# A spectral mixing layer and two gated MLPs in one kernel: the bias added on VectorE, token chunks cut across both batches, waits moved

## The chip, the cores and the metric

One Trainium2 chip; the kernel runs on one core. The metric is the device time of one launch in microseconds (us), the median of the runs shown. Lower is better.

## What is computed

```python
B, N, D, FF = 2, 3008, 256, 1536
X  = np.fft.rfft(x, axis=1)                      # x: (2, 3008, 256)
Yr = X.real @ w_r - X.imag @ w_i + b_r
Yi = X.real @ w_i + X.imag @ w_r + b_i
Yr, Yi = (np.sign(v) * np.maximum(np.abs(v) - 0.01, 0.0) for v in (Yr, Yi))
y  = np.fft.irfft(Yr + 1j * Yi, n=3008, axis=1)  # then 6016 tokens of 256
h  = (sigmoid(y @ w_gate) * (y @ w_val)) @ w_out         # weights in float64
g  = h @ w2_gate
out = (g * sigmoid(g) * (h @ w2_val)) @ w2_out
```

## The kernel before, in words

The transform over 3008 = 47 x 64 positions is done with matmuls in three stages: a 47-point stage, a 64-point stage with the mixing matrices and the shrinkage, and the way back. Nearly every product is done with values split into a high and a low part (three matmuls: high by high, low by high, high by low), with one weight load per matmul.

**First batch** (`spectral_first`, to about 98 us). The 47-point stage ends in `zt`. Then twelve steps run in a software pipeline; step i issues, in this order on TensorE: four transposes of step i+1 (`turn`), the 64-point transform of step i (`forward`), half of the mixing of step i-1 (`mix`), the inverse transform of step i-2 (`inverse`), the other half of `mix`. One half of `mix_of` is 13 matmuls of 256 columns: twelve for the products, and before them one that multiplies a matrix of ones and zeros (`ones`) by a table holding the bias (`bmov`, L239), so that the bias stands in PSUM. `spectrum_parts` splits the spectrum (ScalarE makes the high part, VectorE the low part) and appends the negated first half to each; `shrink_of` then does the shrinkage from PSUM:

```python
nc.scalar.activation(y, pm, AF.Relu, bias=lam)
nc.vector.scalar_tensor_tensor(out=y, in0=pm, scalar=LAM, in1=y, op0=ALU.add, op1=ALU.min)
```

**Weights.** Each of the 12 hidden blocks of a gated MLP arrives as float64 bits (`raw`, three DMAs, two buffers) and is turned into float32 high and low parts by `from_float64`: two ScalarE and seven VectorE operations in five steps (L74 and L75; L77; L80 to L82; L85; L87). `advance(dec)` issues one step. The load of block f+2 is issued after the third step of block f.

**Gated MLPs.** The tokens are cut into chunks: per batch five of 512 and one of 448 columns, 12 in all. A unit is one chunk by one hidden block: `hidden` (12 matmuls into `pg`, then ScalarE `sg`, VectorE `h`, ScalarE `hh`, VectorE `hl`; in the second MLP one more VectorE operation on `sg`) and, two units later, `project` (6 matmuls into `po`). Chunks 0 and 1 of the first MLP go through their blocks in three runs (`TURNS`), while blocks are still being decoded and the rest of the first batch's way back and then the second batch's whole transform (`spectral_second`, one step per unit) run between the units. In the second batch the mixing uses the same `mix_of` and `shrink_of`.

**Order.** Up to the end of the first batch's way back the instructions of each engine stand in program order. From `open_order` on only SP, the queue of nearly all DMAs, keeps program order; the other engines are put in order by the framework's scheduler. Each engine executes its own list strictly in order. At the end, `turn_out` transposes each output chunk and stores it by rows; the last chunk is handled in two pieces, and three of its eight stores are issued by GpSimd (POOL).

Of the kernel before, what the change touches and what calls it, by code (L numbers as in the profile page):

```python
# [37 lines left out]
def tile_kernel(ctx, tc, x, w_r, w_i, b_r, b_i, wts, f1, f2, s2, i1, i1f, eye, one, out):  # L38
# [9 lines left out]
    x2T = [dram.tile([P, 2, N], F32, name=f"x2T{b}") for b in range(B)]  # L48
# [92 lines left out]
    ones = cp.tile([P, P], F32R, name="ones")  # L141
    bmov = cp.tile([P, 256], F32R, name="bmov")
# [3 lines left out]
    def load_tables(fp):  # L146
        wraw = fp.tile([P, 2, 2, 256], F32, tag="wraw", bufs=1, name="wraw")
        braw = fp.tile([P, 256], F32, tag="braw", bufs=1, name="braw")
        nc.gpsimd.memset(braw, 0.0)
        yield  # L150
        nc.sync.dma_start(wraw[:, 0], w_r.rearrange("(k p) e -> p k e", p=P))
        nc.sync.dma_start(wraw[:, 1], w_i.rearrange("(k p) e -> p k e", p=P))
        nc.sync.dma_start(braw[0:33:32, :], b_r.partition_broadcast(2))
        nc.sync.dma_start(braw[1:34:32, :], b_i.partition_broadcast(2))
        nc.sync.dma_start(f2s, f2)
        nc.gpsimd.dma_start(ones, one)
# [8 lines left out]
        nc.vector.tensor_copy(bmov, braw)  # L165
        nc.vector.tensor_tensor(bmov[32:34], braw[32:34], bmov[32:34], op=ALU.subtract)
# [5 lines left out]
    def warm(n):  # L172
        pw = ps_b.tile([P, 512], F32, tag="f", name=f"warm{n}")
        for i in range(n):
            nc.tensor.matmul(pw, idle[:, 0:P], idle, start=True, stop=True)


    def stage1(b, ps, fp, c0=0):
# [4 lines left out]
        def load(c):  # L183
            xr[c] = fp.tile([NJ, 2, 256], F32, tag="xr", bufs=3, name=f"xr{b}_{c}")
            nc.sync.dma_start(xr[c][0:80], xb[0:80, 2 * c:2 * c + 2, :])
            nc.sync.dma_start(xr[c][80:94], xb[80:94, 2 * c:2 * c + 2, :])
# [17 lines left out]
        yield True  # L204
# [16 lines left out]
    def spectrum_parts(b, i, xs, fp, bufs):  # L221
# [6 lines left out]
        nc.vector.tensor_scalar_mul(Xl[:, :, :, 128:192], Xl[:, :, :, 0:64], -1.0)  # L228
# [8 lines left out]
    def mix_of(pm, Xh, Xl, ks):  # L237
        for k in ks:
            ops = [(ones, bmov)]  # L239
# [15 lines left out]
    def spectral_first(zz, ps):  # L255
# [6 lines left out]
        with tc.tile_pool(name="z0", bufs=1, reuse_waits="tile") as z0:  # L262
# [8 lines left out]
            with tc.tile_pool(name="p1", bufs=1, reuse_waits="tile") as fp:  # L271
# [18 lines left out]
                warm(9)  # L290
                next(tables)
                for t, (p0, n) in enumerate(tasks):
# [18 lines left out]
                    if t == 3:  # L311
                        nc.sync.dma_start(eyes, eye)
                        load_table2(0, "s2c", s2, s2c, 2)
                        next(tables)
                        load_table2(0, "i1c", i1f, i1c, 3)
                        next(dec)
                next(tables)
            with tc.tile_pool(name="p2", bufs=1, reuse_waits="tile") as fp:
# [37 lines left out]
                def shrink(i, ks):  # L356
                    shrink_of(Y[i][:, ks], M[i][:, ks])
# [3 lines left out]
                load_table2(1, "s2c", s2, s2c, 2)  # L361
                load_table2(1, "i1c", i1f, i1c, 3)
                for i in range(NS + 1):
# [6 lines left out]
                    if 0 < i < last:  # L370
                        advance(dec, 1 + i % 2)
# [19 lines left out]
    def stage2(b, ps, fz):  # L391
# [20 lines left out]
        def parts(i):  # L412
            X[i] = spectrum_parts(b, i, X[i], fp, 2)
# [5 lines left out]
        def shrink(i):  # L419
            Y[i] = fp.tile([P, KP, 256], F32, tag="y", bufs=1, name=f"y{b}_{i}")  # L420
            shrink_of(Y[i], M.pop(i))
# [125 lines left out]

    pzs = ctx.enter_context(ExitStack())
# [7 lines left out]
    def load_fill(c):  # L556
        xb = x[1].rearrange("(j p) c -> j p c", p=PP)
        x1[c] = pz.tile([NJ, 2, 256], F32, tag="x1", bufs=E1, name=f"x1_{c}")
# [7 lines left out]
    def filled(c, copy):  # L566
        z1 = pz.tile([96, 2, 256], F32, tag="z1e", bufs=2, name=f"z1e_{c}")
# [28 lines left out]
    chunks = []  # L596
    for b in range(B):
        t = 0
        while t < N:
            chunks.append((b, t, min(TC, N - t)))  # L600
            t += TC
    po, turned = {}, []

    def load_x(m, ci):
        b, t0, tn = chunks[ci]
        xin = mp.tile([P, 2, TC], F32, tag="xin", bufs=1, name=f"xin{m}_{ci}")
        nc.sync.dma_start(xin[:, :, :tn], (xT, x2T)[m][b][:, :, t0:t0 + tn])
# [6 lines left out]
    def hidden(m, ci, f):  # L614
        b, t0, tn = chunks[ci]
# [22 lines left out]
    def project(m, ci, f, hh, hl):  # L638
        b, t0, tn = chunks[ci]
# [5 lines left out]
        nt = (tn + 127) // 128  # L645
        for d in range(2):
            for i, (w, v) in enumerate(((wh, hh), (wh, hl), (wl, hh))):
                nc.tensor.matmul(o[d][:, :tn], w[:, 4 + d, :], v[:, :tn],  # L648
                                 start=(first and i == 0), stop=(last and i == 2))
# [6 lines left out]
    def drain(m, ci, f, o):  # L656
        b, t0, tn = chunks[ci]
        nt = (tn + 127) // 128
# [7 lines left out]
        elif ci in part and m == 0:  # L666
# [3 lines left out]
            nc.sync.dma_start(x2T[b][:, :, t0:t0 + tn], xo[:, :, :tn])  # L670
        elif m == 0:
# [3 lines left out]
            nc.sync.dma_start(x2T[b][:, :, t0:t0 + tn], xo[:, :, :tn])  # L675


    def turn_out(ci, o):
        b, t0, tn = chunks[ci]
        end = ci == len(chunks) - 1  # L680
        ot = mp.tile([P, 2, TC], F32, tag="ot", bufs=1, name=f"ot{ci}")
        cut = 256 if end else tn
# [5 lines left out]
        dst = out[b * N:(b + 1) * N, :].rearrange("(j p) c -> p j c", p=PP)  # L688
        ob = mp.tile([P, 4, 256], F32, tag="ob", bufs=RC, name=f"ob{ci}")
        for j in range(0, tn, 256):  # L690
# [6 lines left out]
            for a, k in enumerate(js):  # L697
# [153 lines left out]
```

## Time and profile before

| what | value |
|---|---|
| runs | 1372.14, 1375.63, 1374.31 us; median 1374.31 us |
| profiled execution | 1373.79 us, span in the trace 1372.0 us |
| granted TensorE clock | 0.999 of full speed |
| TensorE (PE) busy | 1358.1 us, 99% of the span, 6814 matmuls |
| VectorE (DVE) busy | 722.1 us, 53% |
| ScalarE (ACT) busy | 536.3 us, 39% |
| GpSimd (POOL) busy | 10.7 us, 1% |
| DMA | 76.09 MB, mean 55 GB/s |

A matmul's recorded duration contains the latency of the array, and successive matmuls overlap; what one of them costs the engine is the distance from its start to the start of the next. A TensorE that is busy 99% can therefore still wait a little between two starts, and only the longer of these waits show as idle time. Each row of a group gives the instructions' busy time, their mean duration in ns, and the idle time of the engine ahead of them with what ended it.

### The profile page before, as it was taken

To read this page: it belongs to the slowest core of one execution; us is meant where nothing else is said; L and a number is where in the kernel's file an instruction comes from. 1 tells how busy PE (TensorE), PEld (TensorE's weight loads), DVE (VectorE), ACT (ScalarE), POOL (GpSimd) and SP (SyncE) were. 2 spreads that over 40 slices of the span, in tenths; PEclk is the share of its full clock that TensorE was granted. 3 is DMA by queue.
4 is the path that set the end of the run, shared out by engine and by line. 5 is a ranking of instruction groups with operands and counts; after the bars stand their busy time and mean duration, and the time that the engine had idled before them with its cause. 6 is when DMAs were issued, how large, how long until landed. Compare 5 with 4: busy or idle time off the path is not lost.

```text
span 1372.0 us, 16931 instructions
## 1 busy us (share of the span) xinstructions
PE 1358.1 (99%) x6814; PEld 1159.4 (85%) x6814; DVE 722.1 (53%) x1099; ACT 536.3 (39%) x941; POOL 10.7 (1%) x25
## 2 busy tenths in 40 slices
PE   9999999999999999999999999999999999999998
PEld 8988878998888888888888888888889888888887
DVE  3648884444334864633335755455555555555554
ACT  4655554444333443433233433333333333333332
POOL 0000000000000000000000000000000000000000
PEclk9999999999999999999999999999999999999999
DMA  7313333333232321000003001001101100100100
GB/s 206 99 56 109 119 111 112 94 108 112 88 109 81 100 75 53 25 31 31 0 29 100 29 1 31 20 13 31 29 0 32 29 4 27 31 11 21 29 15 15
DMA packets 59519, 76.09 MB, mean 55 GB/s; under 512 B 5769, under 2 KB 40632, under 8 KB 59441
## 3 DMA queue, kind: packets, MB, share of 16 engines
q1 hardware_dynamic: 57313, 71.51, 17.2%
q0 software_dynamic: 2128, 3.51, 1.2%
q8 instruction: 53, 0.87, 0.3%
q14 instruction: 25, 0.20, 0.0%
HBM read 51.27 MB, written 23.72 MB: 55 GB/s over the span
## 4 chain that ended last, share of the span: by engine, by line
PE 91%; DMA 3%; DVE 3%; ACT 1%; SPq 1%; issue 1%; POOL 0%; DVEq 0%; POOLq 0%; ACTq 0%
PE pg L623 52%; PE po L648 25%; PE pm L246 5%; PE p L489 2%; PE p L234 2%; PE p L297 1%; DMA raw<-in_moe_w_out_dram 1%; PE pt L696 1%; PE pi L343 1%; DMA xr<-in_x_dram 1%; PE pi L436 1%; PE p L478 1%; DMA xin<-x2T 1%; DMA xin<-xT 0%; PE p L211 0%
## 5 line engine op out<-in xcount | busy, mean ns | idle before, releaser
L623 PE MATMUL pg<-fxh,wh 128*128 128x512 f32 (+1 forms) x1152 | 447.0, 388 | 2.0 <-DVE h L631 1.0
L623 PE MATMUL pg<-fxh,wl 128*128 128x512 f32 (+1 forms) x1152 | 444.1, 386 | 2.1 <-DVE wl L87 2.1
L623 PE MATMUL pg<-fxl,wh 128*128 128x512 f32 (+1 forms) x1152 | 444.2, 386 | 0.0
L627 ACT ACTIVATE sg<-pg 128x512 f32<-128x512 f32 (+1 forms) x288 | 169.0, 587 | 358.0 <-PE pg L623 357.8
L634 ACT CAST hh<-h 128x512 fp32r<-128x512 f32 (+1 forms) x288 | 175.9, 611 | 309.4 <-DVE h L631 308.7
L631 DVE TENSOR_TENSOR h<-sg,pg 128x512 f32<-128x512 f32 (+1 forms) x288 | 194.3, 675 | 188.8 <-ACT sg L627 183.9
L636 DVE TENSOR_TENSOR hl<-h,hh 128x512 fp32r<-128x512 f32 (+1 forms) x288 | 195.6, 680 | 156.1 <-ACT hh L634 154.7
L623 PEld LDWEIGHTS pg<-fxh,wh 128*128 128x128 f32 x1152 | 216.4, 188 | 44.0 <-DVE h L631 2.5
L623 PEld LDWEIGHTS pg<-fxh,wl 128*128 128x128 f32 x1152 | 216.3, 188 | 43.1 <-DVE wl L87 2.5
L623 PEld LDWEIGHTS pg<-fxl,wh 128*128 128x128 f32 x1152 | 216.4, 188 | 38.7
L648 PE MATMUL po<-hh,wh 128*128 128x512 f32 (+1 forms) x576 | 223.9, 389 | 1.0 <-DVE part L661 0.9
L648 PE MATMUL po<-hl,wh 128*128 128x512 f32 (+1 forms) x576 | 222.1, 386 | 0.0
L648 PE MATMUL po<-hh,wl 128*128 128x512 f32 (+1 forms) x576 | 222.1, 386 | 0.0
L629 DVE TENSOR_TENSOR sg<-sg,pg 128x512 f32<-128x512 f32 (+1 forms) x144 | 97.3, 676 | 160.3 <-ACT sg L627 159.9
L648 PEld LDWEIGHTS po<-hh,wh 128*128 128x128 f32 x576 | 108.1, 188 | 21.3 <-DVE part L661 1.3
L648 PEld LDWEIGHTS po<-hh,wl 128*128 128x128 f32 x576 | 108.1, 188 | 20.4
L648 PEld LDWEIGHTS po<-hl,wh 128*128 128x128 f32 x576 | 108.2, 188 | 19.8 <-DVE hl L636 0.4
L246 PE MATMUL pm<-wmh,Xl 128*128 128x256 f32 x192 | 53.7, 280 | 0.0
L246 PE MATMUL pm<-wml,Xh 128*128 128x256 f32 x192 | 53.7, 280 | 0.0
L246 PE MATMUL pm<-wmh,Xh 128*128 128x256 f32 x192 | 53.6, 279 | 0.0
L251 DVE SCALAR_TENSOR_TENSOR y<-pm,y 128x512 f32<-128x512 f32 (+1 forms) x25 | 16.8, 670 | 59.7 <-ACT y L250 59.7
L612 DVE TENSOR_TENSOR fxl<-xin,fxh 128x512 fp32r<-128x512 f32 (+1 forms) x44 | 28.5, 676 | 25.8 <-ACT fxh L611 25.8
(97 smaller groups left out, 852.8 us busy)
## 6 DMA issues: line engine op xcount, KB each, us to landing
raw<-in_moe_w_gate_dram SPq DMA_DIRECT2D x24, 256.0 KB
raw<-in_moe_w_val_dram SPq DMA_DIRECT2D x24, 256.0 KB
raw<-in_moe_w_out_dram SPq DMA_DIRECT2D x24, 256.0 KB
xin<-x2T SPq DMA_DIRECT2D x10, 512.0 KB
xT<-xo SPq DMA_DIRECT2D x26, 188.0 KB
xin<-xT SPq DMA_DIRECT2D x8, 512.0 KB
x2T<-xo SPq DMA_DIRECT2D x8, 512.0 KB
i1s<-in_tab_i_dram POOLq DMA_DIRECT2D x12, 256.0 KB, 4.1
```

The costliest lines, as they stand in the source:

```text
L234: nc.tensor.matmul(pt[:, k, d, :], z[:, k, d * P:(d + 1) * P], s[:, k, :], start=True, stop=True)
L246: nc.tensor.matmul(pm[:, k, :], a, w, start=(j == 0), stop=(j == len(ops) - 1))
L251: nc.vector.scalar_tensor_tensor(out=y, in0=pm, scalar=LAM, in1=y, op0=ALU.add, op1=ALU.min)
L489: nc.tensor.matmul(pt[:, d, q * NJ:(q + 1) * NJ], z[:, q, d * P:(d + 1) * P], f2s, start=True, stop=True)
L612: nc.vector.tensor_tensor(xl[:, k, :tn], xin[:, k, :tn], xh[:, k, :tn], op=ALU.subtract)
L623: nc.tensor.matmul(pg[:, s, :tn], w[:, 2 * s + k, :], v[:, k, :tn], start=(i == 0), stop=(i == 5))
L627: nc.scalar.activation(sg[:, :tn], pg[:, 0, :tn], AF.Sigmoid)
L629: nc.vector.tensor_tensor(sg[:, :tn], sg[:, :tn], pg[:, 0, :tn], op=ALU.mult)
L631: nc.vector.tensor_tensor(h[:, :tn], sg[:, :tn], pg[:, 1, :tn], op=ALU.mult)
L634: nc.scalar.copy(hh[:, :tn], h[:, :tn])
L636: nc.vector.tensor_tensor(hl[:, :tn], h[:, :tn], hh[:, :tn], op=ALU.subtract)
L648: nc.tensor.matmul(o[d][:, :tn], w[:, 4 + d, :], v[:, :tn], start=(first and i == 0), stop=(last and i == 2))
```

## The change

1. **Bias.** The matmul of `ones` by `bmov` is gone from `mix_of` (48 in all), with both tables. A tile `bias` is filled by four DMAs on POOL's queue, and `shrink_of` first adds it on VectorE into a new tile `t` in SBUF; ScalarE and VectorE then work from `t`. In the first batch one decode step is issued between the addition and the rest.
2. **Low part.** In the first batch GpSimd negates the low part, in the second VectorE as before.
3. **Chunks.** They run over the 6016 tokens of both batches: eleven of 512 and one of 384. Chunk 5 takes 448 columns of the first and 64 of the second batch. The array between the two MLPs is stored by chunk.
4. **Loads.** The tables of the 64-point stage have one buffer more and are loaded earlier; two more pieces of the second batch's input are loaded ahead of time, and its transform begins one unit earlier.
5. **Decoding.** In the first ten units three steps per unit instead of two and three in turn.
6. **Ends.** Five warming matmuls at the start instead of nine. In the very last projection the products with the low part go last; the last chunk's first piece is 128 columns; all last stores are on SP.

```diff
 def mix_of(pm, Xh, Xl, ks):
     for k in ks:
-        ops = [(ones, bmov)]
+        ops = []
...
-def shrink_of(y, pm):
-    nc.scalar.activation(y, pm, AF.Relu, bias=lam)
-    nc.vector.scalar_tensor_tensor(out=y, in0=pm, scalar=LAM, in1=y, op0=ALU.add, op1=ALU.min)
+def shrink_of(y, pm, fp, name, ks=slice(0, KP), between=lambda: None):
+    t = fp.tile([P, KP, 256], F32, tag="t", bufs=1, name=f"t{name}")[:, ks]
+    nc.vector.tensor_tensor(t, pm, bias[:, ks], op=ALU.add)
+    between()
+    nc.scalar.activation(y, t, AF.Relu, bias=lam)
+    nc.vector.scalar_tensor_tensor(out=y, in0=t, scalar=LAM, in1=y, op0=ALU.add, op1=ALU.min)
...
-        nc.vector.tensor_scalar_mul(Xl[:, :, :, 128:192], Xl[:, :, :, 0:64], -1.0)
+        neg.tensor_scalar_mul(Xl[:, :, :, 128:192], Xl[:, :, :, 0:64], -1.0)
...
-                    if 0 < i < last:
-                        advance(dec, 1 + i % 2)
+                    if 0 < i < last and i % 2:
+                        advance(dec)
...
-                        shrink(i - 1, slice(1, 2) if i > last else slice(0, 2))
-                    if i % 2 == 0 and 1 < i < last - 2:
-                        load_table2(i // 2 + 1, "s2c", s2, s2c, 2)
-                        load_table2(i // 2 + 1, "i1c", i1f, i1c, 3)
+                        if i > last:
+                            shrink(i - 1, slice(1, 2))
+                        else:
+                            shrink(i - 1, slice(0, 2), lambda: advance(dec, i < last))
+                    if i in (2, 4, 6):
+                        load_table2(i // 2 + 2, "s2c", s2, s2c, 3)
+                        load_table2(i // 2 + 2, "i1c", i1f, i1c, 4)
...
+    chunks = [(g, min(TC, B * N - g)) for g in range(0, B * N, TC)]
+    x2T = [dram.tile([P, 2, tn], F32, name=f"x2T{ci}") for ci, (_, tn) in enumerate(chunks)]
...
-        for d in range(2):
-            for i, (w, v) in enumerate(((wh, hh), (wh, hl), (wl, hh))):
-...
+        ops = [(d, w, v) for d in range(2) for w, v in ((wh, hh), (wh, hl), (wl, hh))]
+        if (m, ci, f) == units[-1]:
+            ops.sort(key=lambda op: op[2] is hl)
...
-                    advance(dec, 1 + u % 2)
+                    advance(dec, 2 if u < 10 else 1 + u % 2)
+                    if u in (4, 5):
+                        load_fill(E1 + u - 4)
...
-                warm(9)
+                warm(5)
```

The order of the instructions moves at three places. The first is VectorE in the twelve steps of the first batch, around the shrinkage of step 5 (`pm_0_5` is its mixed spectrum, `Xl0_6` and `Xl0_7` are low parts, `d_g0_1` and `d_l0_1` belong to the decoding of block 1). Before:

```order
L226 TENSOR_TENSOR Xl0_6_615<-p2_0_6_609,Xh0_6_614 128x4x128
L228 TENSOR_SCALAR Xl0_6_615<-Xl0_6_615 128x4x64
L81 TENSOR_SCALAR d_g0_1_459<-d_a0_1_577 128x768
L82 SCALAR_TENSOR_TENSOR d_l0_1_576<-raw0_1_199,d_g0_1_459 128x768
L251 SCALAR_TENSOR_TENSOR y0_5_621<-pm_0_5_620,y0_5_621 128x512
```

and in the change:

```order
L224 TENSOR_TENSOR Xl0_6_628<-p2_0_6_622,Xh0_6_627 128x4x128
L249 TENSOR_TENSOR t0_5_0_665<-pm_0_5_633,bias_88 128x512
L83 TENSOR_SCALAR d_g0_1_491<-d_a0_1_589 128x768
L84 SCALAR_TENSOR_TENSOR d_l0_1_588<-raw0_1_210,d_g0_1_491 128x768
L252 SCALAR_TENSOR_TENSOR y0_5_634<-t0_5_0_665,y0_5_634 128x512
```

The negation has left VectorE, the addition has come, and the two decode operations stand now between the addition and the last operation of the shrinkage. The same pair stands there for step 8, L76 and L77 (before: L74 and L75) for steps 0 and 7, and a single decode operation for the others up to step 9.

The second place is SP's queue in the same stage, with the tables `s2c` (forward) and `i1c` (inverse) and the raw weights. Before:

```order
L103 DMA raw0_2_454<-in_moe_w_gate_dram 128x2x256
L104 DMA raw0_2_454<-in_moe_w_val_dram 128x2x256
L105 DMA raw0_2_454<-in_moe_w_out_dram 128x512
L268 DMA s2c3_537<-in_tab_s2_dram 128x512
L268 DMA i1c3_539<-in_tab_i1f_dram 128x512
L103 DMA raw0_3_638<-in_moe_w_gate_dram 128x2x256
L104 DMA raw0_3_638<-in_moe_w_val_dram 128x2x256
L105 DMA raw0_3_638<-in_moe_w_out_dram 128x512
L268 DMA s2c4_663<-in_tab_s2_dram 128x512
```

and in the change:

```order
L269 DMA s2c3_427<-in_tab_s2_dram 128x512
L269 DMA i1c3_429<-in_tab_i1f_dram 128x512
L105 DMA raw0_2_466<-in_moe_w_gate_dram 128x2x256
L106 DMA raw0_2_466<-in_moe_w_val_dram 128x2x256
L107 DMA raw0_2_466<-in_moe_w_out_dram 128x512
L269 DMA s2c4_550<-in_tab_s2_dram 128x512
L269 DMA i1c4_552<-in_tab_i1f_dram 128x512
L105 DMA raw0_3_670<-in_moe_w_gate_dram 128x2x256
```

Table 4 stood behind the raw weights of block 3 and stands now ahead of them; in the same way table 3 has passed block 2.

The third place is VectorE in the run of chunk 0 over blocks 7 to 11 (`h0_0_9` and `hl0_0_9` belong to the unit of chunk 0 and block 9, `wl0_10` ends the decoding of block 10, `xl1_6` is a low part in the second batch's first stage). Before:

```order
L85 TENSOR_TENSOR d_a0_10_1874<-d_a0_10_1874,wh0_10_1871 128x768
L631 TENSOR_TENSOR h0_0_9_1942<-sg0_0_9_1940,pg0_0_9_1927 128x512
L87 TENSOR_TENSOR wl0_10_1872<-d_a0_10_1874,d_l0_10_1873 128x768
L192 TENSOR_TENSOR xl1_7_1970<-xr1_7_1907,xh1_7_1969 94x512
L636 TENSOR_TENSOR hl0_0_9_1945<-h0_0_9_1942,hh0_0_9_1944 128x512
```

and in the change:

```order
L87 TENSOR_TENSOR d_a0_10_1817<-d_a0_10_1817,wh0_10_1814 128x768
L636 TENSOR_TENSOR h0_0_7_1883<-sg0_0_7_1881,pg0_0_7_1868 128x512
L89 TENSOR_TENSOR wl0_10_1815<-d_a0_10_1817,d_l0_10_1816 128x768
L191 TENSOR_TENSOR xl1_6_1907<-xr1_6_1848,xh1_6_1906 94x512
L641 TENSOR_TENSOR hl0_0_7_1886<-h0_0_7_1883,hh0_0_7_1885 128x512
```

Block 10 is ready two units earlier: behind `h` of block 7 instead of block 9.

## Rows read from the trace of the kernel before

**Rows 1.** The page, busy time of each engine: us, share of the span, instructions.

```profile
PE 1358.1 (99%) x6814; PEld 1159.4 (85%) x6814; DVE 722.1 (53%) x1099; ACT 536.3 (39%) x941; POOL 10.7 (1%) x25
```

**Rows 2.** The chain of waits, one step of the first batch: start, us, what.

```profile
47.54 1.52 PE pm L246 x13
49.06 0.44 PE pt L325 x4
49.50 0.89 PE p L234 x8
```

**Rows 3.** The same, `hidden` of a 512-column and of a 448-column unit.

```profile
500.40 2.72 PE pg L623 x12
...
758.38 2.43 PE pg L623 x12
```

**Rows 4.** Groups by line: busy us, mean ns | idle before, releaser.

```profile
L82 DVE SCALAR_TENSOR_TENSOR d_l<-raw,d_g 128x768 f32<-128x768 uint32 x24 | 22.9, 956 | 0.6
...
L250 ACT ACTIVATE y<-pm,lam 128x512 f32<-128x512 f32 (+1 forms) x25 | 16.8, 671 | 43.1 <-PE pm L246 43.1
L251 DVE SCALAR_TENSOR_TENSOR y<-pm,y 128x512 f32<-128x512 f32 (+1 forms) x25 | 16.8, 670 | 59.7 <-ACT y L250 59.7
L226 DVE TENSOR_TENSOR Xl<-p,Xh 128x512 fp32r<-128x512 f32 x24 | 16.6, 692 | 8.4 <-ACT Xh L225 8.3
...
L246 PE MATMUL pm<-bmov,ones 128*128 128x256 f32 x48 | 15.7, 327 | 0.0
...
L81 DVE TENSOR_SCALAR d_g<-d_a 128x768 int32<-128x768 int32 x24 | 13.3, 554 | 0.1
...
L228 DVE TENSOR_SCALAR Xl<-Xl 128x256 fp32r<-128x256 f32 x24 | 7.1, 294 | 0.8
...
L149 POOL MEMSET braw<- 128x256 f32 x1 | 0.3, 338 | 0.0
```

**Rows 5.** Waits of TensorE: total us, times, longest us.

```profile
PE pg L623 <- DVE wl L87: 2.1, 1, 2.1
PE pg L623 <- DVE h L631: 1.0, 2, 0.6
PE po L648 <- DVE part L661: 0.9, 1, 0.9
...
PE p L234 <- DMA s2c<-in_tab_s_dram: 0.7, 1, 0.7
PE p L234 <- DMA s2s<-in_tab_s_dram: 0.4, 1, 0.4
```

**Rows 6.** Instructions in order of time, SP's queue: issue, us, tile.

```profile
54.53 0.47 SPq L105 DMA_DIRECT2D raw<-in_moe_w_out_dram  x1
55.09 0.38 SPq L268 DMA_DIRECT2D s2c<-in_tab_s_dram  x1
```

**Rows 7.** The same, ScalarE ahead of the longest waits.

```profile
178.17 0.89 ACT L68 ACTIVATE d_g<-raw 128x768 f32<-128x768 f32 x1 [3.40 <-DMA raw<-in_moe_w_out_dram]
```

**Rows 8.** Busy us of PE, PEld, DVE, ACT, POOL; granted clock, DMA share, GB/s.

```profile
98.00:150.00 52.00, 51.64 (x285) 44.13 (x286) 39.60 (x60) 25.08 (x43) 1.44 (x2) 1.00 0.36 111
150.00:195.00 45.00, 41.99 (x183) 33.34 (x183) 40.74 (x61) 23.35 (x39) 0.00 (x0) 1.00 0.44 133
...
765.00:770.00 5.00, 5.00 (x27) 4.63 (x26) 4.97 (x9) 2.29 (x4) 0.00 (x0) 1.00 0.00 0
```

**Rows 9.** Instructions in order of time, start of the kernel.

```profile
1.19 4.02 PE L175 MATMUL warm<-idle 128*128 128x512 bf16 x9 [1.19 <-DVE idle L289]
...
1.31 0.65 POOL L284 DMA_DIRECT2D f1f<-in_tab_f_dram  x1 [0.45 <-issue]
```

**Rows 10.** The DMAs of tile `f1f`, from issue to landing.

```profile
DMA to landing us min/median/max: 2.8/2.8/2.8
```

**Rows 11.** The chain of waits at the end.

```profile
1362.35 0.57 ACT hh L634
...
1362.97 1.76 PE po L648 x6
```

More of the change, by code (lines that the diff above doesn't have):

```diff
@@ L37, in tile_kernel @@
 @with_exitstack
-def tile_kernel(ctx, tc, x, w_r, w_i, b_r, b_i, wts, f1, f2, s2, i1, i1f, eye, one, out):
+def tile_kernel(ctx, tc, x, w_r, w_i, b_r, b_i, wts, f1, f2, s2, i1, i1f, eye, out):
     nc = tc.nc
@@ L140, in tile_kernel @@
     wml = cp.tile([P, 2, 2, 256], F32R, name="wml")
-    ones = cp.tile([P, P], F32R, name="ones")
-    bmov = cp.tile([P, 256], F32R, name="bmov")
+    bias = cp.tile([P, KP, 256], F32, name="bias")
     lam = cp.tile([P, 1], F32, name="lam")
@@ L147, in load_tables @@
         wraw = fp.tile([P, 2, 2, 256], F32, tag="wraw", bufs=1, name="wraw")
[L148 to L150 removed]
         nc.sync.dma_start(wraw[:, 0], w_r.rearrange("(k p) e -> p k e", p=P))
         nc.sync.dma_start(wraw[:, 1], w_i.rearrange("(k p) e -> p k e", p=P))
[L153 to L154 removed]
         nc.sync.dma_start(f2s, f2)
[L156 removed]
+        for k in range(KP):
+            nc.gpsimd.dma_start(bias[0:64, k], b_r.partition_broadcast(64))
+            nc.gpsimd.dma_start(bias[64:128, k], b_i.partition_broadcast(64))
         nc.gpsimd.dma_start(f1s, f1[:, 0:2])
@@ L595, in tile_kernel @@
     late_ps.append(ps_f)
[L596 to L601, printed above, removed]
     po, turned = {}, []
     def load_x(m, ci):
-        b, t0, tn = chunks[ci]
+        g0, tn = chunks[ci]
         xin = mp.tile([P, 2, TC], F32, tag="xin", bufs=1, name=f"xin{m}_{ci}")
-        nc.sync.dma_start(xin[:, :, :tn], (xT, x2T)[m][b][:, :, t0:t0 + tn])
+        if m:
+            nc.sync.dma_start(xin[:, :, :tn], x2T[ci])
+        else:
+            for b in range(B):
+                lo, hi = max(g0, b * N), min(g0 + tn, (b + 1) * N)
+                if lo < hi:
+                    nc.sync.dma_start(xin[:, :, lo - g0:hi - g0], xT[b][:, :, lo - b * N:hi - b * N])
         yield
@@ L614, in hidden @@
     def hidden(m, ci, f):
-        b, t0, tn = chunks[ci]
+        g0, tn = chunks[ci]
         wh, wl = blocks[m, f]
@@ L644, in project @@
         o = po[0]
-        nt = (tn + 127) // 128
-        for d in range(2):
-            for i, (w, v) in enumerate(((wh, hh), (wh, hl), (wl, hh))):
-                nc.tensor.matmul(o[d][:, :tn], w[:, 4 + d, :], v[:, :tn],
-                                 start=(first and i == 0), stop=(last and i == 2))
+        ops = [(d, w, v) for d in range(2) for w, v in ((wh, hh), (wh, hl), (wl, hh))]
+        if (m, ci, f) == units[-1]:
+            ops.sort(key=lambda op: op[2] is hl)
+        for i, (d, w, v) in enumerate(ops):
+            nc.tensor.matmul(o[d][:, :tn], w[:, 4 + d, :], v[:, :tn],
+                             start=(first and d not in [q for q, _, _ in ops[:i]]),
+                             stop=(last and d not in [q for q, _, _ in ops[i + 1:]]))
         if last and m:
@@ L741, in tile_kernel @@
             turned.pop(0)
-        if len(pend) > 2:
+        if 2 < len(pend) and u + 1 < len(units):
             project(*pend.pop(0))
```

67 lines of the change are left out of this document (31 added, 36 removed).

## The prediction

> **What bounds the kernel now.** I read the page's busy times first: TensorE is busy 99% of the span, VectorE 53% [rows 1]. Busy is not the same as full, so the chain of waits comes next. In the first batch it runs through TensorE's own pieces one behind the other: half a mixing, four transposes, a transform [rows 2]; in the MLPs, where most of the time goes, it is 12 matmuls of `hidden` in 2.72 us [rows 3]. So the spacing of matmuls sets the time, 0.227 us for 512 columns, 0.2025 us for 448 (2.43 / 12), 0.117 us for the 256 of the mixing (1.52 / 13 [rows 2]). The third view is what TensorE waited for: only a handful of waits longer than a few tenths exist, 5.1 us together in the five lines shown [rows 5]. Hence an edit can gain in two ways only: fewer or shorter matmuls, or one of these waits; and it loses wherever a longer way through VectorE and ScalarE reaches TensorE.
>
> **The change part by part.** The sum is made against the profiled execution, 1373.79 us (1372.0 us of span and 1.8 us around it); the median of the runs is 0.5 us above it.
>
> *Bias matmuls.* 48 go, the line of `bmov` [rows 4]. The row's mean of 327 ns is latency; what each costs is one spacing, 0.117 us. In the first batch 24 x 0.117 = 2.8 us, in the second again 2.8 us. The Trainium skill (TensorE: Matmul & The Clock Gate, Back-to-back issue gap) gives an isolated gap of columns divided by 2.4 GHz plus 2.5 ns, 109 ns for 256 columns, and adds that weight loads share in setting it. By that rule both savings would be 5.2 us together instead of 5.6; the trace's spacing decides.
>
> *The longer shrinkage, first batch.* Before, ScalarE read PSUM at once. Now VectorE adds first. Nearest row for that addition, the same engine reading 128x512 from PSUM: 0.69 us; then 0.67 on ScalarE and 0.67 on VectorE [rows 4]; a matmul's result stands 0.2 us after its slot (327 ns recorded against 117 of spacing), and a hand-over takes 0.05 (1362.92 to 1362.97 [rows 11]), so the result is there 2.4 us after the mixing ends. The inverse transform that reads it starts after four transposes, a transform and half a mixing: 0.44 + 0.89 + 12 x 0.117 = 2.73 us [rows 2]. That hides the chain with 0.35 us to spare. But a decode step is now issued between the addition and the last operation. One of 0.95 us outlasts ScalarE's part by 0.25: still hidden. The pair of steps 5 and 8, 0.55 + 0.96 [rows 4], outlasts it by 0.8: late by 0.45, twice. At the end of the stage the cover shrinks: without transposes 2.29 us against 2.65 (late by 0.35), then half a mixing alone, 1.40 against 2.4 (late by 1.0, of which 0.2 was so before), and once more 0.25 in the last half. Sum +2.4. Bounds: 0, if reading SBUF is faster than these rows, and +5.3, if all twelve are late by 0.45. In the second batch at least a unit (18 x 0.227) and a mixing (24 x 0.117), 6.9 us, lie between a mixing and its inverse, so nothing is late; VectorE's 12 x 0.69 us more are spread over twelve such stretches.
>
> *GpSimd's negation.* No row shows GpSimd computing. Nearest rows: its memset of 128x256, 0.34 us, and VectorE's negation of the same shape, 0.29 us [rows 4]. From the end of a transform to the mixing that uses it a whole step passes (half a mixing, an inverse like the transform, half a mixing, transposes, the next transform: 1.40 + 0.89 + 1.40 + 0.44 + 0.89 = 5.0 us), and four matmuls (0.5) before the negated low part is read; making the low part takes 0.2 + 0.69 and as much again on ScalarE ahead of it, 1.7: 3.8 us of cover. Only the very first mixing follows at once; I take 0.4 us late (0 to 1).
>
> *Tables.* Table 4 waits in SP's queue behind the raw weights, leaves at 55.1 us [rows 6], and TensorE waits 0.7 us for it [rows 5]. It now stands ahead of them: -0.7. The wait for `s2s` is queue order too: -0.4.
>
> *Units 14 to 18.* VectorE is busy 40.7 of 45 us there and 39.6 of 52 ahead of it [rows 8]. ScalarE stands 3.4 us at a weight conversion whose DMA is late [rows 7]; `sg` queues behind it, then `h`, the partial sums and `wl`; TensorE waits 0.9 and 2.1 us [rows 5]. Three decode steps in the first ten units fill idle time of the earlier stretch and bring block 10 two units ahead. Full gain 3.0, none at worst; I take -2.5, because the same waiting conversion still stands twice in ScalarE's order. If the decoding is still late, what is late next is `wl` of block 11.
>
> *Chunks.* Columns and matmuls are the same in number, 432 in each chunk. What changes is 448 + 448 + 10 x 512 into 384 + 11 x 512. For 384 the line through 256 and 448 gives 0.174 us, that through 448 and 512 0.178. With these 12 chunks become 1.9 us shorter or the same (432 x 0.0043); I take -1.0. The gap rule of the Trainium skill named above is straight in columns. By that rule the new cut is worth nothing. Chunk 5 is now full; two waits for `h` of 1.0 us together [rows 5] stood at such 448-column units: -0.6 (0 to 1.0). Against that, in the last chunk of the first MLP three blocks are decoded while VectorE is full already, 4.97 of 5 us [rows 8], with units of 3.65 us (18 x 0.2025). They become 3.17 us (18 x 0.176); over seven units that is 3.4 us less cover for VectorE work which shrinks by under 1: +0.7 (0 to 2).
>
> *Start.* Nine warming matmuls take 4.02 us, 0.447 each, twice the spacing for 512 columns later [rows 3, 9]: the array runs at the pace of the lower of its two levels (1.2 GHz), which the granted clock of the profile, 0.999 over the span, does not show. Four fewer would give 1.8 us, but the table `f1f`, issued at 1.31 us [rows 9], lands 2.8 us later [rows 10], so products can begin at 4.1 instead of 5.0. At half speed these 0.9 us are worth 0.4: -0.4. Bounds -0.9, and +0.8 if the full pace comes later by what the four dropped matmuls took. The four bias loads join the DMAs of this stretch; they are needed only behind the first mixing.
>
> *End.* The last six products took 1.76 us [rows 11] for 6 x 0.2025 = 1.2; with the low part last most of that 0.5 goes, and one pair of transposes with it (0.2). Stores from SP alone: nothing. -0.7 (-1.2 to +0.5).
>
> Sum: -2.8 +2.4 +0.4 -0.7 -2.8 -0.4 -2.5 -1.0 -0.6 +0.7 -0.4 -0.7 = -8.4, so 1373.8 - 8.4 = 1365.4; the runs' median would give 1365.9. I say **1365.5 us**. With every term at its good end about -14.7 (1359), at its bad end +3.
>
> **Rivals.** *Late weights stay* (chance 0.15): VectorE is as full as before in units 14 to 18, where nothing was taken from it, and in the 384-column chunk it is overrun. Then 2.5 is not gained and 1.3 more lost: 1369.3, still faster. For it speaks rows 8, against it the 12 us that stand idle on VectorE from 98 to 150.
>
> *VectorE paces the first batch* (0.15): all twelve shrinkages are late, +2.9 beyond the sum. The Trainium skill speaks for it (GPSIMD Engine Reference, Key points and 4.1: ordinary elementwise work belongs on VectorE, and the two share SBUF interfaces, with contention when VectorE has two SBUF inputs); no row here shows both at work. Worked out as a mechanism of this kernel: the last operation now reads `t` and `y`, two SBUF inputs, and the negation falls on it; if each holds it for the length of a 0.34 us memset, 12 x 0.34 = 4.1 more. Then 1365.5 + 2.9 + 4.1 = 1372.5: no change. Against it: VectorE has its 0.29 us per step back.
>
> *GpSimd is slow* (0.05): a negation longer than its 3.8 us of cover holds every mixing. It eats the whole gain from 3.8 + 8.4 / 12 = 4.5 us; at 5.5 us the kernel is at 1365.5 + 12 x 1.7 = 1386, slower. Against it: that is sixteen times its memset row.
>
> That the change does not do what it says is out: in the order the 48 matmuls are gone and table 4 and block 10 stand earlier.
>
> **How the numbers follow.** 0.3% of this kernel, 4.1 us, is about what a measurement can tell from no change. The forecast's own case, from -4 to -14, has 0.65; with the late weights 0.80 faster; the second rival 0.15 same; the third 0.05 slower. The range leaves out the extreme good end and reaches into the second rival: 1360 to 1371.
>
> **What would show it.** Right: mixing rows x12 at 1.40 us; no wait for `s2c`; waits for `wl` and partial sums gone or under 1 us; a few waits of the inverse transform for `y` of 0.3 to 1 us; first products near 4.1 us; POOL's negations under 1 us. Wrong: any repeated wait of the mixing for `Xl`, waits for `y` in every step, or new waits for `h` between 740 and 775 us above 2 us in all.

## The result and the profile after

The changed kernel takes 1380.64 us (median of 4 runs, 1379.71 to 1381.57) against 1373.22 us for the kernel before (4 runs, 1371.25 to 1375.63): a ratio of 1.0051, 95% interval 1.0035 to 1.0066. It is slower by 7.4 us; forecast were 1365.5 us and a range of 1360 to 1371. The sign was wrong.

The two profiled executions have spans of 1372.0 and 1378.3 us. Cut at the same points of the program (starts of the first matmul of each), they differ as follows; the last column adds up the prediction's terms for that stretch.

| stretch | before, us | after, us | difference | forecast |
|---|---|---|---|---|
| start to the first mixing | 24.60 | 37.47 | **+12.87** | -0.4 |
| to the first `hidden` | 73.76 | 72.63 | -1.13 | -0.7 |
| to unit 48 (with the second batch's transform) | 282.45 | 278.29 | -4.16 | -5.7 |
| to the second MLP (unit 144) | 392.00 | 389.09 | -2.91 | -0.4 |
| to the last transposes | 591.96 | 590.12 | -1.84 | -1.2 |
| to the end | 7.23 | 10.70 | **+3.47** | 0 |
| sum | 1372.0 | 1378.3 | +6.30 | -8.4 |

Four stretches went roughly as the sum said, 10.0 us gained where 8.0 were forecast. (0.6 of the 10.0 is owed to the late start: ahead of the first `hidden` TensorE waits 0.87 us for a copy, `z1e`, in the kernel before and in e1 below, and in all 0.23 us in the change.) Two rows at the ends, which the prediction had put at -0.4 and at nothing, took 16.3 us. The first: instructions of TensorE in order of time at the start (start us, us, what, idle time ahead of it and its releaser). The kernel before:

```profile
5.01 15.72 PE L297 MATMUL p<-f1f,xr 94*128 94x128 f32 x128
20.56 0.27 PE L325 MATMUL pt<-eyes,zt 128*128 128x128 f32 x1
```

and the change:

```profile
1.17 2.32 PE L171 MATMUL warm<-idle 128*128 128x512 bf16 x5 [1.17 <-DVE idle L290]
4.26 27.98 PE L297 MATMUL p<-f1f,xr 94*128 94x128 f32 x128 [0.78 <-DMA f1f<-in_tab_f_dram]
32.04 0.42 PE L325 MATMUL pt<-eyes,zt 128*128 128x128 f32 x1
```

The products begin at 4.26 us, as forecast (4.1), 0.75 us earlier than before. But the stage, 4.26 to 32.04 us, is 27.8 us long; before it was 15.55. Each of the 128 products takes 0.217 us (27.8 / 128); from start to start nearly all stand 0.213 us apart, where before most stood 0.112 apart. The windows of the same stretch (columns as in [rows 8]) rule out a shortage of data:

```profile
5.00:10.00 5.00, 5.00 (x24) 4.74 (x23) 0.72 (x2) 0.64 (x2) 0.00 (x0) 1.00 0.99 240
10.00:35.00 25.00, 24.80 (x116) 24.18 (x115) 5.57 (x11) 4.82 (x10) 0.00 (x0) 1.00 0.73 216
```

The DMA engines are full up to 10 us and not behind it (0.99, then 0.73), but TensorE is busy without a break, so it lacks no data, and only 116 products pass in 25 us. The granted clock stands at 1.00 all the while. That column is no witness here; the nine warming matmuls of [rows 9] too stood 0.42 us apart (1.19 to 5.01 us) with a mean clock of 0.999. The spacing is the witness: the array ran at the lower of its two levels (1.2 GHz) through the whole stage, and through the first transform behind it (8 matmuls busy 2.08 us in the change, 1.16 before).

The rest of the profile answers to the rows shown of before. The chain of waits in the changed kernel, a first-batch step (to [rows 2]), then a 512-column and a 384-column `hidden` (to [rows 3]):

```profile
46.34 0.44 PE pt L325 x4
46.77 0.89 PE p L232 x8
47.66 1.41 PE pm L244 x12
...
502.83 2.72 PE pg L628 x12
...
742.96 2.08 PE pg L628 x12
```

Half a mixing is 1.41 us instead of 1.52, one spacing less; 384 columns take 2.08 / 12 = 0.173 us. Waits of TensorE (total us, times, longest), to [rows 5]:

```profile
PE pm L244 <- DVE Xl L224: 1.1, 1, 1.1
PE pi L343 <- PE pm L244: 0.9, 1, 0.9
PE p L297 <- DMA f1f<-in_tab_f_dram: 0.8, 1, 0.8
...
PE pi L343 <- DVE y L252: 0.5, 2, 0.3
PE pm L244 <- POOL Xl L226: 0.3, 1, 0.3
```

The waits for `wl`, for the partial sums, for `h` and for `s2c` are gone. New are late inverses (`pi`, 1.4 us together), one mixing of the second batch that waits for its low part (1.1 us) and one for GpSimd. Groups by line, to [rows 4]:

```profile
L251 ACT ACTIVATE y<-t,lam 128x512 f32<-128x512 f32 (+1 forms) x25 | 17.7, 708 | 55.8 <-DVE t L249 55.8
L249 DVE TENSOR_TENSOR t<-pm,bias 128x512 f32<-128x512 f32 (+1 forms) x25 | 16.8, 670 | 47.1 <-PE pm L244 47.0
...
L226 POOL TENSOR_SCALAR Xl<-Xl 128x256 fp32r<-128x256 f32 x12 | 12.2, 1017 | 74.4 <-DVE Xl L224 74.4
```

The bias costs VectorE 0.67 us a step, as taken; GpSimd's negation takes 1.02 us in the mean, three times its memset.

### The profile page after: what moved, and what is told of

Read it like the earlier page. It is cut to its first block, busy times and chain, and to the rows that moved or that the text cites. A ratio compares the mean times of both kernels' runs of the same rounds, so it can differ in the third digit from the quotient of the medians.

```text
span 1378.3 us, 16872 instructions
## 1 busy us (share of the span) xinstructions
PE 1362.1 (99%) x6760; PEld 1161.1 (84%) x6760; DVE 734.0 (53%) x1109; ACT 537.6 (39%) x941; POOL 22.4 (2%) x36
## 4 chain that ended last, share of the span: by engine, by line
PE 94%; issue 2%; DMA 1%; DVE 1%; ACT 0%; SPq 0%; POOL 0%; POOLq 0%; DVEq 0%; ACTq 0%
PE pg L628 55%; PE po L654 28%; PE pm L244 4%; PE p L493 2%; PE p L232 1%; PE pi L343 1%; PE pt L702 1%; PE p L209 1%; PE pi L440 1%; PE p L482 1%; DMA xr<-in_x_dram 0%; DMA xin<-xT 0%; PE pt L325 0%; DMA s2s<-in_tab_s_dram 0%; DVE y L252 0%
## 5 line engine op out<-in xcount | busy, mean ns | idle before, releaser
L249 DVE TENSOR_TENSOR t<-pm,bias 128x512 f32<-128x512 f32 (+1 forms) x25 | 16.8, 670 | 47.1 <-PE pm L244 47.0
L251 ACT ACTIVATE y<-t,lam 128x512 f32<-128x512 f32 (+1 forms) x25 | 17.7, 708 | 55.8 <-DVE t L249 55.8
```

The costliest lines, as they stand in the source:

```text
L249: nc.vector.tensor_tensor(t, pm, bias[:, ks], op=ALU.add)
L251: nc.scalar.activation(y, t, AF.Relu, bias=lam)
```

## The experiments

They are kernels e1 to e13 and e15; medians, and ratios to the kernel before timed in the same job.

### What the start costs: e1 to e4

**e1**, the change with nine warming matmuls:

```diff
-                warm(5)
+                warm(9)
```

> The changed kernel with nine warming matmuls again. Theory A (the first stage ran at the array's lower pace because the warming was cut): the first mixing starts at about 24.7 us instead of 37.5, the 128 products of the first stage stand 0.12 us apart instead of 0.214, and the time is 1380.6 - 12.8 = 1367.8 us. Theory B (the start is worth under 1 us, as the prediction had it, and the loss lies in waits of the longer shrinkage, GpSimd or the chunks): 1379.8 to 1381 us.

Measured: 1369.29 us (5 runs, 1368.92 to 1369.63), ratio 0.9964 (0.9951 to 0.9976). **e2** is the kernel before with `warm(9)` replaced by `warm(5)`, nothing else:

> The kernel before with five warming matmuls and nothing else changed. Theory A: the first stage takes 27.8 us instead of 15.5, the time is about 1373.2 + 12.5 = 1385.7 us. Theory B: 1372.8 us, 0.4 less than before.

Measured: 1386.86 us (4 runs), ratio 1.0088 (1.0073 to 1.0103); the 128 products took 27.7 us. Four matmuls that compute nothing are worth about 12 us in either kernel (by the ratios, 1.0051 against 0.9964 in the one and 1.0088 in the other). The start of e1:

```profile
1.17 4.02 PE L171 MATMUL warm<-idle 128*128 128x512 bf16 x9 [1.17 <-DVE idle L290]
4.99 4.84 PE L297 MATMUL p<-f1f,xr 94*128 94x128 f32 x32
10.42 2.02 PE L297 MATMUL p<-f1f,xr 94*128 94x128 f32 x16 [0.59 <-DMA xr<-in_x_dram]
12.82 9.34 PE L297 MATMUL p<-f1f,xr 94*128 94x128 f32 x80 [0.38 <-DMA xr<-in_x_dram]
```

Now 80 products take 9.2 us (12.82 to 22.00), 0.115 each, and TensorE even waits for x. The four matmuls filled the time until `f1f` landed and 0.7 us more. (The pace rose only in the products: in e1, e5, e6 and the kernel before, where they follow the warming at once, the first 6 to 10 still stood 0.213 us apart and the rest 0.112.) Was it their number, or the idle time that they filled? **e3** has nine of them, and three memsets on GpSimd ahead of the load of `f1f`, which bring the idle time back:

```diff
+                nc.gpsimd.memset(bias, 0.0)
+                nc.gpsimd.memset(bias, 0.0)
+                nc.gpsimd.memset(bias, 0.0)
...
-                warm(5)
+                warm(9)
```

> Nine warming matmuls, but the table of the first products is loaded about 1.9 us later (three memsets ahead of it on GpSimd), so that TensorE stands still for about 1 us between the warming and the products. If the idle gap is what kept the lower pace: products 0.21 us apart, about 1381 us. If the length of the unbroken warming is what counts: products soon 0.12 us apart, about 1369 us.

Measured: 1380.78 us, one run. **e4** is the change with `warm(7)`:

> The changed kernel with seven warming matmuls, which end when the table lands, so that there is hardly a gap. If the gap is what kept the lower pace: products 0.12 us apart for most of the stage, about 1367.5 us. If too little warming did: still 0.21 us apart, about 1380.6 us.

Measured: 1380.36 us, one run. In both the pace had risen and was lost again. TensorE in e3, then in e4:

```profile
6.61 26.57 PE L300 MATMUL p<-f1f,xr 94*128 94x128 f32 x128 [1.75 <-issue]
...
1.18 3.17 PE L171 MATMUL warm<-idle 128*128 128x512 bf16 x7 [1.18 <-DVE idle L290]
4.38 2.02 PE L297 MATMUL p<-f1f,xr 94*128 94x128 f32 x16
8.24 8.02 PE L297 MATMUL p<-f1f,xr 94*128 94x128 f32 x36 [1.84 <-DMA xr<-in_x_dram]
```

In e3 the first ten products behind the gap stand 0.112 us apart and all others 0.213. In e4 the first 16 products are fast (0.126 us each). Then the faster start has run out of x; TensorE stands 1.84 us, and behind that gap a product takes 0.22. Waits for x of 0.3 to 1.3 us in the profiles of e1, e5, e6 and e7 did not end the pace. Once the clock has fallen, the column shows it. Windows of e4:

```profile
5.00:10.00 5.00, 3.16 (x21) 3.00 (x20) 0.72 (x2) 0.64 (x2) 0.00 (x0) 0.76 1.00 244
10.00:35.00 25.00, 24.80 (x116) 24.18 (x115) 5.58 (x11) 4.58 (x10) 0.00 (x0) 0.50 0.72 214
```

These are the 116 products of the changed kernel in the same 25 us, with a granted clock of 0.50 beside them; e3 has 0.50 there too, after 1.75 us of idle time.

### What brings the pace back: e8 and e13

**e8** is the change with nine more of the same 512-column matmuls after 64 of its products:

```diff
+                    if t == 4:
+                        pw = bank("dense")
+                        for _ in range(9):
+                            nc.tensor.matmul(pw, idle[:, 0:P], idle, start=True, stop=True)
```

> The change (five warming matmuls), and nine more of the same 512-column matmuls in the middle of the first stage, after 64 of its 128 products. Theory A, dense wide matmuls raise the pace and the 128-column products hold it: the second 64 products at 0.11 us instead of 0.214, 6.6 us less, for 3.7 us more: 1377.7 us. Rival B, nothing in the first stage raises it: nine at 0.43 us more, 1384.5 us. Rival C, it rises, but the products let it fall again: between the two, with a granted clock that comes and goes in 10 to 35 us.

Measured: 1377.21 us, one run. TensorE in e8:

```profile
8.89 10.58 PE L297 MATMUL p<-f1f,xr 94*128 94x128 f32 x48 [0.66 <-DMA xr<-in_x_dram]
19.26 0.63 PE L314 MATMUL dense<-idle 128*128 128x512 bf16 x1
20.12 2.20 PE L314 MATMUL dense<-idle 128*128 128x512 bf16 x7 [0.22 <-issue]
22.15 7.31 PE L297 MATMUL p<-f1f,xr 94*128 94x128 f32 x64
```

48 products took 10.4 us ahead of the wide matmuls, 64 took 7.15 behind them (22.15 to 29.30), 0.112 each. So products of 128 columns hold the pace, but in this kernel they had not raised it. **e13** starts the five of the change later, so that no idle time lies between them and the products:

```diff
-                nc.vector.memset(idle, 0.0)
+                for _ in range(5):
+                    nc.vector.memset(idle, 0.0)
```

> The change as it is, with four more memsets of 0.27 us ahead of the five warming matmuls, so that they end when the table f1f has landed (4.3 us) and the products follow at once. Theory A, five are too few, and products of 128 columns raise nothing: 0.214 us each as in the change, 1380.6 us. Rival B, the idle 0.78 us did it: the pace rises within the first products and stays, 0.11 us each, some 12 us less, 1368.5 us.

Measured: both. Of 8 executions four took 1368.2 to 1370.2 us and four 1380.6 to 1382.7. The profiled one is one of the slow ones:

```profile
4.85 27.73 PE L298 MATMUL p<-f1f,xr 94*128 94x128 f32 x128
```

No idle time stands ahead of its products, and all run at the lower level; that the four fast ones ran at the upper one is read from their times alone. So without the gap five are enough in some executions; with it they were in none (4 runs of the change, 4 of e2). The gap counts, but it is not the whole cause. What decides from one execution to the next no row shows.

### What the end costs: e5 and e6

The last seven stores of the change all go through SP's queue. **e5** is e1 with the stores dealt out as before:

```diff
+                    dma = nc.gpsimd if end and r and k in (0, 256) else nc.sync
-                    nc.sync.dma_start(dst[pcol // PP, pcol % PP, jj:jj + step, :], ob[r:r + step, k // 128, :])
+                    dma.dma_start(dst[pcol // PP, pcol % PP, jj:jj + step, :], ob[r:r + step, k // 128, :])
```

> Nine warming matmuls, and the stores of the last chunk dealt out as before (three of seven from GpSimd's queue). In the kernel with nine warming matmuls 6.9 us pass from the last store's issue to the end, 3.7 us before the change; from 1362 to 1366 us its DMA share is 0.13 to 0.14, the work of two of the 16 engines. Theory A, the two 94-row stores on one queue end on two DMA engines: the tail is again as before, 3.1 us less, 1366.2 us. Rival B, the tail is only the count of issues on SP at 0.34 us each: three fewer there, 1368.3 us.

Measured: 1366.63 us (12 runs), ratio 0.9949 (0.9936 to 0.9963), 2.7 us below e1; last transposes to the end 6.9 us (1357.96 to 1364.9), e1 10.6. **e6** leaves all on SP, but cuts each store of 94 rows into 80 and 14 (`cut = 80 if end and step == 94 else step`, and a second store for the rest):

> Nine warming matmuls, all stores from SP, but each 94-row store of the last chunk cut into 80 and 14 rows: two more issues. Theory A (rows of 94 go to two DMA engines): of 248 KB on two engines 60 KB are left, and at the 45 GB/s of the stretch from 1362 to 1366 us that is some 4 us less, less 0.7 for two issues: 1366 to 1367 us, and no stretch with a DMA share of 0.13. Rival B (count of issues): 0.7 us more, 1370.0 us.

Measured: 1366.87 us (12 runs; 1365.9 without the three that are told of below), ratio 0.9968 (0.9944 to 0.9992), with two issues more; last transposes to the end 7.6 us (1355.63 to 1363.2). So it was not the count of issues. Windows of e1 over its last stores:

```profile
1361.00:1362.00 1.00, 0.00 (x0) 0.00 (x0) 0.00 (x0) 0.00 (x0) 0.00 (x0) 0.90 0.57 121
1362.00:1363.00 1.00, 0.00 (x0) 0.00 (x0) 0.00 (x0) 0.00 (x0) 0.00 (x0) 0.50 0.14 49
1363.00:1364.00 1.00, 0.00 (x0) 0.00 (x0) 0.00 (x0) 0.00 (x0) 0.00 (x0) 0.50 0.13 40
1364.00:1365.00 1.00, 0.00 (x0) 0.00 (x0) 0.00 (x0) 0.00 (x0) 0.00 (x0) 0.50 0.14 48
```

and of e6:

```profile
1360.00:1361.00 1.00, 0.00 (x0) 0.00 (x0) 0.00 (x0) 0.00 (x0) 0.00 (x0) 1.00 0.57 181
1361.00:1362.00 1.00, 0.00 (x0) 0.00 (x0) 0.00 (x0) 0.00 (x0) 0.00 (x0) 0.70 0.09 29
1362.00:1363.20 1.20, 0.00 (x0) 0.00 (x0) 0.00 (x0) 0.00 (x0) 0.00 (x0) 0.50 0.00 0
```

A share of 0.13 to 0.14 of 16 engines is two engines. For some 4 us two of them work off what is left at 40 to 49 GB/s together, and with 80 + 14 rows that stretch is gone. The Trainium skill (DMA: Bandwidth & Descriptors, Why a DMA increments its semaphore by 16 and not by 1) says that a transfer runs on the largest number of engines, up to 16, that divides its outer size; for 94 rows that is two. The trace agrees, with its 0.14. In e5, where GpSimd's queue has the two stores of 94 rows, no such stretch shows either; a window over its last stores:

```profile
1361.00:1362.00 1.00, 0.00 (x0) 0.00 (x0) 0.00 (x0) 0.00 (x0) 0.20 (x1) 0.96 0.78 234
```

One run of e5 (1377.5 us) and three of e6 (1378.9 to 1379.9) lie 11 to 13 us above the others, with a mean granted clock of 0.988 to 0.990 where the others have 0.998 or 0.999; e3 and e4 had 0.988 and 0.987. That points to the loss of pace of e4, in the wait for x: with nine warming matmuls it still happens now and then.

### The smaller terms: e7 and e9 to e12, and all together: e15

**e7** is e1 with the four bias loads behind table 0 in SP's queue instead of at the head of GpSimd's (the same four lines, moved):

> Nine warming matmuls, and the four bias loads moved off GpSimd's queue at the start, behind table 0 in SP's queue. Theory A: they took DMA time from the x loads, for which TensorE waited 1.0 us; the first mixing starts at 24.6 us as before the change, not 26.0: 1367.9 us. Rival B, the x loads are late for another reason: 1369.3 us, waits for xr still 1.0 us.

Measured: 1368.30 us (5 runs), ratio 0.9955 (0.9943 to 0.9967). The wait for x is still 1.3 us in its profile, and 0.4 and 1.4 us in e6 and e5, which have the loads at the start: it differs from run to run, and the loads are not what decides it. Nor is the 1.0 us below e1 shown to be the loads' work. The profiled execution of e7 starts its first mixing 1.3 us earlier than that of e1 (24.73 us; e6, with the loads at the start, 24.63), and loses 1.3 us again between units 48 and 144. That loss lies in chunk 5 of the first MLP (units 60 to 71), which no edit of e1 to e15 touches but in which profiles differ: its twelve units of 4.08 us take 48.97 us in the change and 48.98 in e1, but 50.32, 50.25 and 50.00 in e5, e7 and e9, where TensorE waits for `h`. A line of e5's waits:

```profile
PE pg L628 <- DVE h L636: 0.7, 2, 0.5
```

Differences of about 1 us between two kernels below are therefore read by stretch, and not put down to an edit as a whole. **e9** adds e5's stores and `warm(14)` to e7:

> The change with fourteen warming matmuls, the bias loads behind table 0 in SP's queue, and the last chunk's stores on two queues as before. Five more at full pace are 5 x 0.227 = 1.1 us, so products begin at 6.1 us, when more of x is there. Theory A: no wait for xr is left, the first mixing starts at 6.1 + 14.6 + 4.1 = 24.8 us instead of 26.0, the pace is never lost (none of the runs near 1378), and against the 1366.6 us of the stores on two queues it is 1365.4 us. Rival B, the five only come on top, and the waits stay: 1367.7 us.

Measured: 1366.02 us (5 runs, 1365.21 to 1366.23), ratio 0.9939 (0.9925 to 0.9952). No wait for x is left, the 128 products take 14.3 us, the first mixing starts at 24.77 us, and no run lost the pace; it is 0.6 us below e5, not 1.2. On this base, **e10** issues the first batch's decode step behind the shrinkage:

```diff
-                            shrink(i - 1, slice(0, 2), lambda: advance(dec, i < last))
+                            shrink(i - 1, slice(0, 2))
+                            advance(dec, i < last)
```

> The kernel of the run before, with the decode step of the first batch issued behind the shrinkage instead of between its addition and its last operation. Theory A, the step in between makes the inverses of steps 5 and 8 late: their 0.37 and 0.34 us go, and some 0.2 near the end of the stage, 0.8 us less than the run before; the 1.1 us at the very end stay. Rival B, VectorE is late by itself: no change.

Measured: 1364.03 us (5 runs), ratio 0.9926 (0.9913 to 0.9938): 2.0 us less, more than expected. VectorE in e9 around step 5:

```profile
53.89 0.69 DVE L246 TENSOR_TENSOR t<-pm,bias 128x512 f32<-128x512 f32 x1 [1.84 <-PE pm L241]
54.50 0.55 DVE L83 TENSOR_SCALAR d_g<-d_a 128x768 int32<-128x768 int32 x1
55.08 0.96 DVE L84 SCALAR_TENSOR_TENSOR d_l<-raw,d_g 128x768 f32<-128x768 uint32 x1
55.96 0.68 DVE L249 SCALAR_TENSOR_TENSOR y<-t,y 128x512 f32<-128x512 f32 x1
```

and in e10:

```profile
53.50 0.69 DVE L246 TENSOR_TENSOR t<-pm,bias 128x512 f32<-128x512 f32 x1 [1.39 <-PE pm L241]
54.98 0.69 DVE L249 SCALAR_TENSOR_TENSOR y<-t,y 128x512 f32<-128x512 f32 x1 [0.79 <-ACT y L248]
```

From the addition to the last operation 2.07 us pass in e9 and 1.48 in e10. The inverse of that step starts 1.85 us after the half mixing ahead of it starts in e9 and 1.49 in e10, the one of step 8 1.81 and 1.49: 0.68 us. With what follows each of them the stretch from the first mixing to the first `hidden` is 0.92 us shorter (73.33 and 72.41 us), near the 0.8 expected. The rest isn't shown to be the edit's: 0.4 is an earlier start of the products (6.06 against 6.44 us; the five kernels with fourteen warming matmuls start them between 5.88 and 6.79 us), 0.4 lies in chunk 5, and 0.2 in the stretch to unit 48, where the second batch waits 0.6 us for `Xl` instead of 1.2, which I can't explain, and 0.4 for `s2s`. **e11** is e9 with the first batch's negation on VectorE (`nc.gpsimd` becomes `nc.vector` in `forward`):

> The same kernel as the first of these runs, with the first batch's negation on VectorE again (0.29 us a step) instead of GpSimd (1.02 us). Theory A, it is hidden on either engine: 0.3 us less at most, from the one wait of the first mixing for GpSimd. Rival B, VectorE paces the first batch and the move relieved it: 12 x 0.29 = 3.5 us more than the first of these runs.

Measured: 1364.51 us (5 runs), ratio 0.9928 (0.9916 to 0.9941). The first mixing is 3.11 us long instead of 3.72; the transposes and the transform behind it take 0.17 us longer, the others are as before, and the inverses are no later. That leaves 0.47 us less in the first batch's stretch; 1.0 us of the difference to e9 is chunk 5 (49.04 against 50.00 us). GpSimd's negation stood on the path once, at the first mixing. What the two engines did to each other the trace of e9 shows:

```profile
52.14 0.85 POOL L223 TENSOR_SCALAR Xl<-Xl 128x256 fp32r<-128x256 f32 x1 [3.74 <-DVE Xl L221]
57.33 1.49 POOL L223 TENSOR_SCALAR Xl<-Xl 128x256 fp32r<-128x256 f32 x1 [4.34 <-DVE Xl L221]
...
57.16 0.95 DVE L87 TENSOR_TENSOR d_a<-d_a,wh 128x768 f32<-128x768 f32 x1
```

Eight of the twelve negations took 0.85 to 0.86 us; the four that ran beside decode operations of VectorE took 1.09, 1.30, 1.49 and 1.49. On VectorE two of those operations were 0.07 us longer than in e11 (1.03 and 0.64 us instead of 0.96 and 0.56), the others not. None of it reached TensorE. **e12** is e9 with the decode pace of before (`advance(dec, 1 + u % 2)`):

> The same kernel as the first of these runs, with the decode pace of before in the first ten units (one or two steps a unit instead of two). Theory A, the third step per two units is what brings block 10 in time: the wait for wl comes back at units 17 and 18, 3.7 us more than the first of these runs. Rival B, the decode steps of the first batch and the earlier loads did it: no change.

Measured: 1368.73 us (5 runs), ratio 0.9957 (0.9945 to 0.9970): 2.7 us more; in the profiles units 16 to 18 take 3.5 us more than in e9, and chunk 5 1.0 less. Waits of TensorE in e12:

```profile
PE pg L628 <- DVE wl L89: 1.7, 1, 1.7
...
PE po L654 <- ACT wh L82: 0.7, 1, 0.7
```

**e15** puts e10 and e11 together:

> Fourteen warming matmuls, bias loads late, stores on two queues, the decode step behind the shrinkage, and the first batch's negation on VectorE. Theory A, the gains measured apart add up: the first mixing 0.6 us shorter than in the run with the decode step moved alone (3.1 instead of 3.7 us), 1363.4 us. Rival B, without GpSimd the VectorE of the first batch is late again, 0.7 us of late inverses: 1364.1 us.

Measured: 1363.84 us (5 runs, 1363.06 to 1364.10), ratio 0.9918 (0.9905 to 0.9932). That is 0.2 us below e10, less than the 0.6 of the first mixing (3.13 us in its profile). Neither account covers that: behind the shorter mixing the transform now waits for its table and starts 0.5 us later,

```profile
PE p L229 <- DMA s2c<-in_tab_s_dram: 0.3, 1, 0.3
```

and two steps lose 0.12 us each at their inverse, so the first batch's stretch is no shorter than in e10 (72.65 and 72.41 us). It is the fastest here: 0.8% below the kernel before, 1.2% below the change (16.8 us).

## Why the prediction was wrong

**The step that failed is "Start".** It read correctly that nine warming matmuls ran at the lower level and that the profile's clock doesn't show it, and forecast the first product (4.1 us, measured 4.26). Then it took the pace as something that comes a fixed time later: "at half speed these 0.9 us are worth 0.4", +0.8 at worst. The runs showed a switch: the stage runs at full pace but for its first products (15.6 us in e6) or at the lower (27.8), and five matmuls with 0.78 us of idle time behind them leave it at the lower for all 128 products. The worst case should have been the whole stage at the warming matmuls' pace [rows 9]: up to its own 15.55 us again. That is a rival on the slower side, and it was not among the three. The term is -0.4 forecast, +12.9 measured.

**The second is in "End":** "Stores from SP alone: nothing." It priced the issues and not the DMA engines. Measured +3.5. The rest of that term, low part last, gave nothing: the starts of the last six products span 0.99 us instead of 1.38, but with 384 columns TensorE waits 0.56 us for `hh` ahead of them instead of 0.16. That the second MLP is 1.84 us shorter up to the last transposes, forecast 1.2 with its half of the chunks, is mostly the chunks' spacing (1.1 us) and a wait for `h` that went (0.6).

Without these two the sum would have been near: e5 and e6, which take both back, measured 1366.6 and 1366.9 us, and 1365.5 + 0.4 = 1365.9 was forecast for that. By its other steps:

- *Bias matmuls*: right. Half a mixing is one spacing shorter in every step of the first batch, and a step of the second batch 0.23 us shorter (8.83 to 8.60 us for a unit in e1): 2.8 us each.
- *Longer shrinkage*: right in place and size (forecast +2.4; the parts as written add up to 2.3). In the changed kernel and in e1 the inverses of steps 5 and 8 are 0.36 and 0.32 us late, 0.45 and 0.42 with what follows them (forecast 0.45 each); the end of the stage is 1.6 later (forecast 1.4), 0.5 of it in the last half. e10 showed the cause of the first two. VectorE did not pace the stage: the other inverses are on time.
- *GpSimd*: right in kind, late once, for 0.6 us (forecast 0.4, bounds 0 to 1). The contention that the second rival took from the Trainium skill (GPSIMD Engine Reference, Key points and 4.1) is there in the trace, mostly at GpSimd's cost (0.85 to 1.49 us for a negation), but it reached no step of TensorE; the operation that the rival named, the last of the shrinkage, never ran beside a negation in the change.
- *Tables*: the wait for `s2c` is gone, 0.9 us with what followed it; the one for `s2s` only in part, 0.2 us left (0.3 in e1).
- *Units 14 to 18*: forecast -2.5. In e1 the starts of units 16 and 19 move from +1.64 to -2.02 us against before: -3.7. e12 showed that the third decode step makes most of it (3.5 us). Against that, the second batch's 1.1 us wait for `Xl` was not foreseen, where the sum said that nothing is late. That VectorE's 0.69 us more per step are its cause is not shown: no run takes them away, and in e1 VectorE stands idle twice for 0.69 us in the 4 us before it, waiting for ScalarE.
- *Chunks*: forecast -1.0, -0.6 and +0.7. The spacing for 384 columns is 0.173 us, lower than the 0.174 to 0.178 of the two lines: 432 x (2 x 0.2025 - 0.2267 - 0.1733) = 2.2 us. The waits for `h` went in the change, but in chunk 5 they come and go with the profile: 1.4 us in e5 and 1.3 in e7 (e7 above). The +0.7 of the 384-column chunk did not show. By the gap rule of the Trainium skill (TensorE: Matmul & The Clock Gate, Back-to-back issue gap) the cut is worth nothing; the measurement decides against it.

## What to carry to other kernels

Matmuls that compute nothing at the start are not a cost to be trimmed to the first load: price their removal as the whole following stage at the lower pace, and look for idle time behind them, since after gaps of 1.75 and 1.84 us the full pace was lost here, and the products ran slowly to the end of the stage. Read the pace from the spacing of equal matmuls, not from the clock column, until that has shown a first change. When a small edit changes a median by about 1 us, compare the profiles stretch by stretch before crediting it: about half of what e10 gained and more of what e11 gained lay in stretches that their edits do not touch. And when transfers change queue or shape at the end of a kernel, look at the share of DMA engines that they keep busy, not only at bytes and issues.

## What was not expected of the hardware

- The array's pace at the start came out differently in executions of one and the same kernel: by the times, four and four in e13, 1 in 12 in e5, 3 in 12 in e6; with fourteen warming matmuls it was the same in all 25 runs (e9 to e12, e15).
- In the change 25 us of products, TensorE busy for 24.80 of them, passed at the lower level; in e8 the products behind nine 512-column matmuls (2.9 us, 19.26 to 22.15) ran at the upper one.
- A store of 94 rows from SP kept two of 16 DMA engines busy (share 0.14).
- GpSimd's negation of 128x256 elements takes 0.85 us alone and up to 1.49 beside decode operations of VectorE, VectorE's 0.29 [rows 4].
